# Layer one's second product in groups of 384 tokens over four rooms, with a new order of work

## The chip, the cores and the metric

The kernel runs on one core of a Trainium2 chip. The metric is the device time of one execution in microseconds (us), taken over three runs.

## The reference

Attention of 4 batches, 8 heads, 576 tokens, head size 64; half the heads see a window of 32 tokens, half every fourth token of 128. Its output, 2,304 tokens of 512, goes through two layers of products:

```python
def _moe_ref(x, w_in, w_out, g_ln):
    h = x @ w_in                                   # 2304x512 @ 512x1024
    h_max = np.max(h, axis=-1, keepdims=True)
    e = np.exp(h - h_max)
    sm = e / (np.sum(e, axis=-1, keepdims=True) + 1e-09)
    solu = h * sm
    mu = np.mean(solu, axis=-1, keepdims=True)
    var = np.mean((solu - mu) ** 2, axis=-1, keepdims=True)
    ln = (solu - mu) / np.sqrt(var + 1e-06) * g_ln
    return (ln @ w_out).astype(np.float32)         # 1024x512: the second product of layer one

def _moe2_ref(x, w_in, w_out):
    h = x @ w_in                                   # 512x2048
    g = h * (1.0 / (1.0 + np.exp(-1.702 * h)))
    return (g @ w_out).astype(np.float32)          # 2048x512
```

## The kernel before

Three parts overlap on one core. **Attention** goes by batch, five units of heads and tokens each: scores `s` (L268, with filler matmuls on `ident_b`, L250), softmax `t` on DVE, ACT and POOL, transposes `ptp` (L351), the product with v, `xt` (L381, L384), and copies `xr`. Loads of qk and v (L225, L231) are issued by SP. For two of a batch's units q, k and v lie, until attention ends, in room lent by the tiles `y1`, where layer one's results come later.

**Layer one** goes by tiles of 128 tokens, 18 of them. A tile's x is split into a high and a low fp32r half (`xh`, `xl`); `h` is 2 x 12 matmuls of 512 columns (L522); exp, the sums and the norm run on ACT, DVE and POOL in a tile `e`, of which there are three. Then `moe_lt` (L577) transposes e into PSUM, 2 x 4 matmuls, `moe_lnh` (L585, ACT or DVE) copies the high half out and `moe_lnl` (L588, DVE) subtracts the low one. The weights of layer one come in eight chunks (0 to 3 w_in, 4 to 7 w_out), as 64-bit numbers loaded by `fetch_w1` (L422) into rooms `w1r`, converted on ACT and DVE (L429, L437, L441), and split into `wi_h`, `wi_l` (L478, L491) and `wo_h`, `wo_l` (L485, L495). The rooms `w1r` and the transposed halves `lnh`, `lnl` share four slots "ln".

The second product, `moe_y` (L599), takes groups of YG = 256 tokens, two tiles. For each of 9 groups and 4 blocks `dm` of 128 outputs it makes 24 matmuls into one of four PSUM banks "B":

```python
for f in range(NF1):
    for j, (w, x) in enumerate(((wo_h, lnh), (wo_h, lnl), (wo_l, lnh))):
        nc.tensor.matmul(yps[g, dm][:, 0:n], w[:, f, ds_], x[:, f, 0:n],
                         start=(f == 0 and j == 0), stop=(f == NF1 - 1 and j == 2))
```

`moe_yc` (L604, ACT or DVE) copies the 256 columns into `y1`, tiles of TG = 512 tokens.

**Layer two** takes three passes of 768 tokens, each by seven products of half blocks (`hx`, `hz`, L721; `ox`, `oz`, L799; 384 columns a matmul). Its operands `yc` are sums and splits of pieces of y1 (L697, L704, L708), cut where a piece crosses two y1 tiles. Its weights are fetched while layer one runs, as 64-bit numbers (L629), converted, summed in fours (L638), split (L655, L659), stored to DRAM as `wdq`, `wdo` (L663) and loaded again later as `ws`, `wo`, `w`. A unit of this is listed in PARK: lists 1 and 2 use rooms in y1, list 3 rooms that open when attention has ended (`closed`). Kept units stay in `hl` tiles.

The order is written out. Every step is a work `add(rank, engine, cost, function, after, take, give)`; `in_order` walks the table ORDER, PICKS says which of a step's engines does it, and `emit` ties each engine's instructions to that order. So an engine, and SP's queue of loads, goes by the table, and semaphores between engines decide when each step starts. `plan_sequence` sets which steps follow which at first (`push_lt`, `push_y`), the wait lists `after` and the slots (SLOTS) which must.

Of the kernel before, what the change touches and what calls it, by code (L numbers as in the profile page):

```python
# [8 lines left out]
F32 = mybir.dt.float32  # L9
# [21 lines left out]
TG = 512  # L31
GROUPS = [(g * TG, min(TG, NT - g * TG)) for g in range((NT + TG - 1) // TG)]
NTILE = NT // P
YG = 256
NYG = NT // YG
# [131 lines left out]
def attention_moe_kernel(ctx, tc, qk, qk_last, v, v_last, masks, w_in, w_out, g_ln, w2_in, w2_out, out):  # L167
# [30 lines left out]
    lnp = m1_ctx.enter_context(tc.tile_pool(name="lnp", bufs=4))  # L198
# [393 lines left out]
    def moe_y(g, dm):  # L592
        n = YG
        yps[g, dm] = psB.tile([P, 512], F32, tag="B", name=f"y{g}_{dm}")
        lnh, lnl = lns[g]
        ds_ = slice(dm * P, dm * P + P)
        for f in range(NF1):
            for j, (w, x) in enumerate(((wo_h, lnh), (wo_h, lnl), (wo_l, lnh))):
                nc.tensor.matmul(yps[g, dm][:, 0:n], w[:, f, ds_], x[:, f, 0:n],  # L599
                                 start=(f == 0 and j == 0), stop=(f == NF1 - 1 and j == 2))  # L600

    def moe_yc(g, dm, copy):
        gg, c0 = g * YG // TG, g * YG % TG
        copy(y1[gg][:, dm, c0:c0 + YG], yps.pop((g, dm))[:, 0:YG])  # L604
# [273 lines left out]
    for what, i in LOADS:  # L878
# [12 lines left out]
        else:  # L891
            done["w", i] = add(r, "SP", 2 * W_T * f, lambda i=i: (fetch_w1(i, 0), fetch_w1(i, 1)), lag=2.2, take=("ln",))
# [39 lines left out]
    for c in range(8):  # L932
# [659 lines left out]
```

## Time and profile before

| | |
|---|---|
| median of three runs | 652.5 us (652.29 to 653.0) |
| the profiled execution | 652.41 us |
| its span in the profile | 650.6 us |
| granted clock of TensorE, mean | 0.994 |
| PE busy | 632.1 us, 97% |
| DVE, ACT, POOL busy | 69%, 54%, 45% |
| DMA moved | 163.56 MB, 251 GB/s in the mean |

The page shows one execution. "Busy" adds up an engine's instructions; the slices cut the span into 40 equal parts; the chain goes back from the last instruction, at each step to what released it. PE lines are matmuls, PEld lines loads of weights beside them, SPq lines the issue of transfers by SP. A matmul's record is longer than its distance to the next, since they are pipelined; what a matmul costs PE in a row is read from a run's length by its count.

### The profile page before, as it was taken

The page shows a single profiled execution, that of the slowest core. Times are in us where ns is not written, and L with a number is a line of the kernel's source. Part 1 is how long each engine was busy: PE and PEld are TensorE (multiplying, and loading weights), DVE is VectorE, ACT ScalarE, POOL GpSimd, SP SyncE. Part 2 cuts the span into 40 slices and gives each one's busy share as a digit, 9 for nine tenths or more (in the row PEclk, how much of TensorE's full clock was granted, in tenths as well). Part 3 has the DMA queues.
Part 4 walks back from the last instruction along what each step waited for, and adds up shares of the span by engine and source line. Part 5 has one row for each costly group of instructions (what it writes and reads, how often), then busy time and mean ns, then how long its engine had stood idle before and what let it go on. Part 6 is the DMA issues. An engine that isn't in the chain of part 4 may idle for free.

```text
span 650.6 us, 14875 instructions
## 1 busy us (share of the span) xinstructions
PE 632.1 (97%) x5878; PEld 594.6 (91%) x5878; DVE 448.1 (69%) x778; ACT 351.8 (54%) x766; POOL 292.9 (45%) x338
## 2 busy tenths in 40 slices
PE   6699999999999999999999999999999999999997
PEld 3478788889998989999999999999999999999997
DVE  4978789786846857796878879635477943447573
ACT  4677877755726565445656665333455531435552
POOL 3536563656557365555554215210535550224373
PEclk9989999999999999999999999999999999999999
DMA  8987428654537357877799999757899866779783
GB/s 337 394 287 303 172 85 282 225 168 174 162 128 255 146 174 247 320 230 228 283 346 379 358 329 314 227 198 265 264 295 286 301 221 226 244 245 341 251 255 111
DMA packets 65013, 163.56 MB, mean 251 GB/s; under 512 B 6960, under 2 KB 28592, under 8 KB 64944
## 3 DMA queue, kind: packets, MB, share of 16 engines
q1 hardware_dynamic: 64944, 162.62, 72.7%
q8 instruction: 46, 0.75, 0.5%
q14 instruction: 23, 0.19, 0.1%
HBM read 126.42 MB, written 36.18 MB: 250 GB/s over the span
## 4 chain that ended last, share of the span: by engine, by line
PE 89%; DMA 3%; DVE 3%; ACT 1%; issue 1%; POOL 0%; SPq 0%; POOLq 0%; ACTq 0%
PE y L599 16%; PE h L522 16%; PE hz L721 15%; PE oz L799 14%; PE hx L721 11%; PE ox L799 9%; PE lt L577 3%; PE xt L381 2%; PE ptp L351 1%; PE xt L384 1%; PE s L268 1%; DMA wo<-wdo 1%; DMA ws<-wdq 1%; DVE gs L767 1%; DMA wdo<-hl_('o', 3, 1)_1_5307 1%
## 5 line engine op out<-in xcount | busy, mean ns | idle before, releaser
L764 ACT CAST gs<-g 128x384 fp32r<-128x384 f32 x168 | 85.2, 514 | 70.6 <-PE oz L799 27.3
L767 POOL TENSOR_TENSOR gs<-g,gs 128x384 fp32r<-128x384 f32 x51 | 56.5, 1114 | 112.3 <-ACT gs L764 104.7
L721 PE MATMUL hz<-yc,ws 128*128 128x384 f32 x492 | 97.7, 334 | 0.0
L767 DVE TENSOR_TENSOR gs<-g,gs 128x384 fp32r<-128x384 f32 x117 | 75.3, 663 | 28.9 <-ACT gs L764 28.2
L721 PEld LDWEIGHTS hz<-yc,ws 128*128 128x128 f32 x492 | 86.5, 188 | 0.0
L599 PE MATMUL y<-lnh,wo_h 128*128 128x256 f32 x288 | 82.8, 288 | 0.0
L599 PE MATMUL y<-lnl,wo_h 128*128 128x256 f32 x288 | 81.4, 283 | 0.0
L599 PE MATMUL y<-lnh,wo_l 128*128 128x256 f32 x288 | 81.4, 283 | 0.0
L721 PE MATMUL hx<-yc,ws 128*128 128x384 f32 x369 | 74.9, 335 | 0.3 <-DMA ws<-wdq 0.3
L750 ACT ACTIVATE g<-g 128x384 f32<-128x384 f32 x72 | 36.6, 522 | 58.6 <-DVE g L740 40.6
L760 POOL TENSOR_TENSOR g<-g,g 128x384 f32<-128x384 f32 x34 | 38.5, 1136 | 65.3 <-ACT g L750 41.2
L721 PEld LDWEIGHTS hx<-yc,ws 128*128 128x128 f32 x369 | 64.8, 188 | 0.7 <-ACT hl_('q', 7, 1)_0_4958 L655 0.5
L522 PE MATMUL h<-wi_h,xh 128*128 128x512 f32 x144 | 59.3, 412 | 0.0
L799 PE MATMUL ox<-gs,wo 128*128 128x384 f32 x288 | 55.4, 337 | 1.1 <-DMA wo<-wdo 1.1
L522 PE MATMUL h<-wi_h,xl 128*128 128x512 f32 x144 | 56.4, 391 | 0.0
L522 PE MATMUL h<-wi_l,xh 128*128 128x512 f32 x144 | 56.3, 391 | 0.0
L599 PEld LDWEIGHTS y<-lnh,wo_h 128*128 128x128 f32 x288 | 55.0, 191 | 0.4
L599 PEld LDWEIGHTS y<-lnl,wo_h 128*128 128x128 f32 x288 | 55.1, 191 | 0.3
L799 PE MATMUL oz<-gs,wo 128*128 128x384 f32 x288 | 55.3, 336 | 0.0
L599 PEld LDWEIGHTS y<-lnh,wo_l 128*128 128x128 f32 x288 | 55.1, 191 | 0.0
L799 PE MATMUL oz<-gs,w 128*128 128x384 f32 x288 | 53.6, 337 | 0.5 <-DVE ou L811 0.5
L799 PEld LDWEIGHTS ox<-gs,wo 128*128 128x128 f32 x288 | 50.3, 188 | 1.5 <-DMA wo<-wdo 1.4
(397 smaller groups left out, 1315.8 us busy)
## 6 DMA issues: line engine op xcount, KB each, us to landing
wo<-wdo SPq DMA_DIRECT2D x48, 512.0 KB, 6.4
ws<-wdq SPq DMA_DIRECT2D x41, 512.0 KB, 6.0
w<-wdo SPq DMA_DIRECT2D x72, 256.0 KB, 5.6
ws<-wdq SPq DMA_DIRECT2D x41, 384.0 KB, 5.4
qk<-in_qk_dram SPq DMA_DIRECT2D x14, 528.0 KB, 6.4
v<-in_v_dram SPq DMA_DIRECT2D x14, 512.0 KB, 7.1
y<-in_w_in_dram SPq DMA_DIRECT2D x9, 512.0 KB, 5.1
wdq<-y SPq DMA_DIRECT2D x9, 512.0 KB, 3.9
```

What stands on the lines that cost most here:

```text
L268: nc.tensor.matmul(ps[QB * j:QB * j + QB, h, m * KW:m * KW + KW], q_[rows, c:c + QB], k_[rows, c:c + KW], start=not masked, stop=not maske ...
L351: nc.tensor.transpose(ps[:, j * P:j * P + P], t[:, 2 * j:2 * j + 2, :].rearrange("p m k -> p (m k)"), ident)
L381: nc.tensor.matmul(o, w, pt[rows, x:x + QB].rearrange("p (r t) -> p r t", r=4), start=True, stop=True, tile_position=(64 * par, 64 * h))
L522: nc.tensor.matmul(hps[i][:, half, :], x[:, kt, :], w[:, kt, fs], start=(kt == 0 and j == 0), stop=(kt == KT - 1 and j == 2))
L577: nc.tensor.transpose(ps[:, j, :], es[i][:, f * P:f * P + P], ident)
L599: nc.tensor.matmul(yps[g, dm][:, 0:n], w[:, f, ds_], x[:, f, 0:n], start=(f == 0 and j == 0), stop=(f == NF1 - 1 and j == 2))
L721: nc.tensor.matmul(ps[:, 0:TB2], quad_weights(p, q, m, kk, a), yc2[m][:, x, kk, :], start=(m < 4 and kk == 0 and i == 0), stop=(kk == 1 an ...
L750: nc.scalar.activation(g_tile(q, 0, 0) if (half, b) == (0, 0) else src, src, AF.Gelu_apprx_sigmoid)
L760: eng.tensor_tensor(o_block(jj, *o), o_block(jj, *x), o_block(jj, *y_), op)
L764: nc.scalar.copy(gsp[jj, m][:, 0], o_block(jj, half, b))
L767: eng.tensor_tensor(gsp[jj, m][:, 1], o_block(jj, half, b), f32(gsp[jj, m][:, 0]), ALU.subtract)
L799: nc.tensor.matmul(ps, w, gsp[jj, m][:, x], start=m < 4 and first and i == 0, stop=last and i == 2, skip_group_check=True)
```

## The change

`moe_y` takes groups of TG = 384 tokens, three tiles, so that there are 6 groups and 24 products of 24 matmuls. The transposed halves have one tile `ln_t` of four rooms, each for one tile of 128 tokens, high and low. An even group uses rooms 0, 1, 2, an odd one 3, 2, 1 (`ln_slot`): the first tile of a group goes to the room that the group before leaves out and waits for the group before that; the other two wait for the last product of the group before. The odd groups' tokens so lie in reverse order of tiles; the host turns them round in the output. The matmul's moving operand has 384 columns in three rooms, 128 in each. `ln_t` has the place of `w1_t`, four load slots for the eight chunks of w_in and w_out (`W_ORDER`, `W_SLOT`); the transposes of the first four tiles wait for all eight low halves.

The results lie in six tiles of 384 tokens, four of them in one tile `y1_early`. The lent room and the parked rooms lie in it at other places, list 2 splits into a room `park_hl` of attention's own, and one unit moves from list 2 to list 3. The wait for the units that borrow room goes from the y products to their copies. Layer two's pieces, 384 tokens wide, fall on whole y1 tiles. The tables ORDER and PICKS are new.

```diff
-TG = 512
-YG = 256
-NYG = NT // YG
+TG = 384
+NG = NT // TG
+GT = TG // P
...
-    y1 = {}
-    for g in range(3):
-        y1[g] = cpool.tile([P, KT, TG], F32, name=f"y1_{g}")
+    y1_early = cpool.tile([P, 4, KT, TG], F32, name="y1_early")
+    y1 = {g: y1_early[:, g] for g in range(4)}
...
-    lnp = m1_ctx.enter_context(tc.tile_pool(name="lnp", bufs=4))
+    lnp = m1_ctx.enter_context(tc.tile_pool(name="lnp", bufs=1))
+    w1_t = lnp.tile([P, 4, 2, 512, 2], U32, tag="ln", name="w1_t")
...
+    park_hl = ac.tile([P, 1024], F32R, name="park_hl")
+    parked = {1: (flat[:, 4096:5120], flat[:, 3072:4096].bitcast(F32R)), 2: (flat[:, 5120:6144], park_hl)}
...
-            lns[g] = (lnp.tile([P, NF1, YG], F32R, tag="ln", name=f"lnh{g}"),
-                      lnp.tile([P, NF1, YG], F32R, tag="ln", name=f"lnl{g}"))
+            ln_t = lnp.tile([P, 4, 2, NF1, P], F32R, tag="ln", name="ln_t")
...
-        lnh, lnl = lns[g]
+        lnh, lnl = (ln_t[:, g % 2:g % 2 + GT, which] for which in range(2))
...
-                nc.tensor.matmul(yps[g, dm][:, 0:n], w[:, f, ds_], x[:, f, 0:n],
+                nc.tensor.matmul(yps[g, dm][:, 0:TG].rearrange("p (t n) -> p t n", t=GT), w[:, f, ds_], x[:, :, f, :],
...
-            t = add(r, "PE", 0.37, lambda i=i, h=h2: moe_lt(i, h), [w, lt_of.get(i * P // YG), before_],
-                    take=("B", "ln", "ln") if i % 2 == 0 and h2 == 0 else ("B",), give=("e",) if h2 else ())
+            t = add(r, "PE", 0.37, lambda i=i, h=h2: moe_lt(i, h), [w, before_] + (list(lo.values()) if i <= GT else []), take=("B",),
+                    give=("e",) if h2 else ())
...
-                    + [end[n] for n in range(UB)] + ([closed] if g >= 6 else []) + (ys_ if dm == KT - 1 else []), take=("B",),
-                    give=("ln", "ln") if dm == KT - 1 else ())
+                    + (ys_ if dm == KT - 1 else []), take=("B",))
...
+                            [y] + [end[n] for n in range(UB)] + ([closed] if g == 4 else []), give=("B",), pick=0,
...
+    for i in range(GT, NTILE):
+        g = i // GT
+        free = y_done.get(g - 2 if i % GT == 0 else g - 1)
+        for h2 in range(2 if free else 0):
+            lt_of2[i, h2].after.append(free)
...
-                if k < 3:
+                for g in ((), (2, 3), (3,), ())[k]:
                     for dm in range(KT):
-                        yc[2 * k, dm].after.append(x)
-                        yc[2 * k + 1, dm].after.append(x)
+                        yc[g, dm].after.append(x)
+                if k == 2:
+                    closed.after.append(x)
...
+def ln_slot(i):
+
+    g, k = divmod(i, GT)
+    return 3 - k if g % 2 else k
...
+W_ORDER = (1, 3, 0, 2, 5, 7, 4, 6)
+W_SLOT = {1: 0, 3: 3, 0: 1, 2: 2, 5: 0, 7: 3, 4: 1, 6: 2}
...
-ORDER = [8, 1, 56, 57, 10, 58, 59, 60, 61, 5, 97, 98, 99, 9, 266, 267, 67, 268, 269, 270, 68, 62, 0, 46, 63, 100, 101,
...
-    got = _np.asarray(r.results[0]["out_0_dram"]).reshape(DM, B, 4, S // 4)
-    return _np.ascontiguousarray(got.transpose(1, 3, 2, 0)).reshape(NT, DM)
+    got = _np.array(r.results[0]["out_0_dram"]).reshape(DM, NG, GT, P)
+    got[:, 1::2] = got[:, 1::2, ::-1].copy()
+    return _np.ascontiguousarray(got.reshape(DM, B, 4, S // 4).transpose(1, 3, 2, 0)).reshape(NT, DM)
```

How the order moves, at three places. In these rows a line number is that of the kernel in question; behind it stand the operation, out<-in and the tile.

SP's queue at the start, before (`y_0` to `y_2` are lent rooms in y1, `w1r` the chunks of layer one's weights, `in_v` the v of batch 0):

```order
L222 DMA y_1_78<-in_qk_dram 128x544
L422 DMA w1r_275<-in_w_in_dram 128x1024 x2
L237 DMA qkl_336<-in_qk_last_dram 128x640
L239 DMA vl_338<-in_v_last_dram 128x512
L422 DMA w1r_392<-in_w_in_dram 128x1024 x2
L231 DMA v_420<-in_v_dram 128x1024
L231 DMA v_428<-in_v_dram 128x1024
L422 DMA w1r_446<-in_w_in_dram 128x1024 x2
L225 DMA qk_549<-in_qk_dram 128x1056
L231 DMA y_1_78<-in_v_dram 128x1024
L231 DMA y_2_79<-in_v_dram 128x1024
```

and with the change, where `y_early` are the lent rooms and `w_t` the chunks:

```order
L425 DMA w_t<-in_w_in_dram 128x1024 x2
L228 DMA qk_316<-in_qk_dram 128x1056
L234 DMA y_early<-in_v_dram 128x1024
L425 DMA w_t<-in_w_in_dram 128x1024 x4
L240 DMA qkl_442<-in_qk_last_dram 128x640
L242 DMA vl_444<-in_v_last_dram 128x512
L234 DMA v_450<-in_v_dram 128x1024
L234 DMA v_456<-in_v_dram 128x1024
L234 DMA y_early<-in_v_dram 128x1024
L425 DMA w_t<-in_w_in_dram 128x1024 x2
```

Before, two v loads of batch 0 stood ahead of the fourth w_in chunk (`w1r_446`) and two behind it. Now one stands ahead of the second and third chunk, and all of them ahead of the fourth.

DVE around the first transposes' low halves, before (`wo_l` are the low halves of w_out, `lnl` those of the transposed tiles, `y_1`, `y_2`, parked units under conversion):

```order
L337 TENSOR_SCALAR sx_1318<-sx_1318 128x8
L338 RECIPROCAL sx_1318<-sx_1318 128x8
L588 TENSOR_TENSOR lnl_1215<-lt_0_1216,lnh_1214 128x4x128
L588 TENSOR_TENSOR lnl_1215<-lt_1_1274,lnh_1214 128x4x128
...
L588 TENSOR_TENSOR lnl_1215<-lt_1_1464,lnh_1214 128x4x128
...
L585 CAST lnh_1214<-lt_0_1437 128x4x128
L588 TENSOR_TENSOR lnl_1215<-lt_0_1437,lnh_1214 128x4x128
L441 SCALAR_TENSOR_TENSOR w1r_911<-w1r_911 128x1024
L483 TENSOR_SCALAR wo_h<-w1r_911,g_sb 128x512 x2
L495 SCALAR_TENSOR_TENSOR wo_l<-w1r_827,g_sb,wo_h 128x512 x2
...
L495 SCALAR_TENSOR_TENSOR wo_l<-w1r_911,g_sb,wo_h 128x512 x2
```

and with the change:

```order
L360 COPY pt_1263<-ptp_1241 128x512
L498 SCALAR_TENSOR_TENSOR wo_l<-w_t,g_sb,wo_h 128x512 x4
L444 SCALAR_TENSOR_TENSOR y_early<-y_early 128x512
L498 SCALAR_TENSOR_TENSOR wo_l<-w_t,g_sb,wo_h 128x512 x2
...
L545 SCALAR_TENSOR_TENSOR e_1311,mu_1368<-h_1091,e_1311 128x1024
...
L533 TENSOR_REDUCE nm_1391<-h_1246 128x1
...
L589 TENSOR_TENSOR ln_t<-lt_0_1380,ln_t 128x512
L589 TENSOR_TENSOR ln_t<-lt_1_1429,ln_t 128x512
...
L589 TENSOR_TENSOR ln_t<-lt_1_1386,ln_t 128x512
```

The last four low halves of w_out stood behind the first tiles' low halves; now all of them stand ahead of the first.

PE at the end of layer one, before (of each y product the first matmul is shown; `lt` are the transposes, `hx`, `hz` the first products of layer two):

```order
L577 MATMUL lt_1_4251<-ident,e_3882 128x128 x4
L577 MATMUL lt_1_4259<-ident,e_4069 128x128 x4
L599 MATMUL y_3_4266<-lnh_3978,wo_h 128x256
...
L599 MATMUL y_1_4302<-lnh_4164,wo_h 128x256
...
L599 MATMUL y_0_4340<-lnh_4164,wo_h 128x256
...
L599 MATMUL y_2_4373<-lnh_4164,wo_h 128x256
...
L721 MATMUL hx_0_0_4403<-yc_0_4023,ws_0_0_0_4025 128x384 x3
L721 MATMUL hx_0_0_4403<-yc_0_4023,ws_0_1_0_4074 128x384 x3
L599 MATMUL y_3_4416<-lnh_4164,wo_h 128x256
...
L721 MATMUL hx_0_1_4455<-yc_1_4333,ws_0_0_1_4161 128x384 x3
```

and with the change:

```order
L599 MATMUL y_3_3866<-ln_t,wo_h 128x384 x2
...
L579 MATMUL lt_0_3905<-ident,e_3694 128x128 x4
L579 MATMUL lt_0_3912<-ident,e_3784 128x128 x4
L579 MATMUL lt_1_3918<-ident,e_3784 128x128 x4
L579 MATMUL lt_1_3926<-ident,e_3694 128x128 x4
L720 MATMUL hx_0_0_3931<-yc_0_3810,ws_0_0_0_3864 128x384 x3
L720 MATMUL hx_0_0_3931<-yc_0_3810,ws_0_1_0_3847 128x384 x3
L720 MATMUL hz_0_2_3943<-yc_2_3748,ws_0_0_1_3714 128x384 x3
L720 MATMUL hz_0_2_3943<-yc_2_3748,ws_0_1_1_3854 128x384 x3
L599 MATMUL y_0_3955<-ln_t,wo_h 128x384 x2
...
L599 MATMUL y_1_3992<-ln_t,wo_h 128x384 x2
...
L720 MATMUL hx_0_1_4114<-yc_1_4020,ws_0_0_1_3714 128x384 x3
```

Before, the last product of the group ahead stood behind the last transposes, and layer two's first product between the last two y products. Now the last 16 transposes stand together, 12 matmuls of layer two behind them, and then the last group's four products in a row.

## Rows read from the trace of the kernel before

**Rows 1.** The page: busy time by engine, and what DMA moved in 40 slices of 16.3 us.

```profile
PE 632.1 (97%) x5878; PEld 594.6 (91%) x5878; DVE 448.1 (69%) x778; ACT 351.8 (54%) x766; POOL 292.9 (45%) x338
...
GB/s 337 394 287 303 172 85 282 225 168 174 162 128 255 146 174 247 320 230 228 283 346 379 358 329 314 227 198 265 264 295 286 301 221 226 244 245 341 251 255 111
```

**Rows 2.** The page: the chain that ended last, by engine and by line.

```profile
PE 89%; DMA 3%; DVE 3%; ACT 1%; issue 1%; POOL 0%; SPq 0%; POOLq 0%; ACTq 0%
PE y L599 16%; PE h L522 16%; PE hz L721 15%; PE oz L799 14%; PE hx L721 11%; PE ox L799 9%; PE lt L577 3%; PE xt L381 2%; PE ptp L351 1%; PE xt L384 1%; PE s L268 1%; DMA wo<-wdo 1%; DMA ws<-wdq 1%; DVE gs L767 1%; DMA wdo<-hl_('o', 3, 1)_1_5307 1%
```

**Rows 3.** Stretches: length, busy us (instructions) by engine, granted clock, DMA share, GB/s.

```profile
0.00:50.00 50.00, 37.57 (x964) 25.92 (x965) 35.86 (x58) 31.43 (x78) 20.29 (x21) 0.93 0.93 340
50.00:100.00 50.00, 49.41 (x856) 41.66 (x854) 40.49 (x72) 37.66 (x88) 28.41 (x40) 1.00 0.47 175
150.00:200.00 50.00, 50.00 (x393) 45.94 (x392) 31.65 (x61) 26.35 (x52) 29.18 (x42) 1.00 0.52 180
300.00:350.00 50.00, 49.75 (x287) 49.46 (x286) 37.52 (x73) 26.98 (x55) 27.66 (x31) 1.00 0.89 317
350.00:400.00 50.00, 48.94 (x281) 48.30 (x280) 42.87 (x76) 31.35 (x64) 14.97 (x13) 1.00 1.00 340
```

**Rows 4.** The chain in order of time: start us, us, what, matmuls.

```profile
87.23 1.06 PE xt L384 x64
88.29 2.95 PE h L522 x12
...
258.25 0.44 PE lt L577 x4
...
278.97 11.51 PE y L599 x96
...
330.84 6.33 DMA ws<-wdq
...
372.81 7.65 DMA wo<-wdo
...
387.02 8.32 PE ox L799 x48
```

**Rows 5.** Groups on PE: line, operation, names, shapes, count, busy us, mean ns, idle.

```profile
L599 PE MATMUL y<-lnh,wo_h 128*128 128x256 f32 x288 | 82.8, 288 | 0.0
...
L522 PE MATMUL h<-wi_h,xl 128*128 128x512 f32 x144 | 56.4, 391 | 0.0
```

**Rows 6.** Timeline of PE: the filler matmuls before a masked score.

```profile
26.74 1.04 PE L250 MATMUL s<-ident_b 128*128 128x512 bf16 x4
```

**Rows 7.** Timeline at the start: start us, us, engine, line, operation, [idle, releaser].

```profile
27.64 1.22 ACT L437 ACTIVATE w1r<-w1r 128x1024 uint32<-128x1024 uint8 x1
...
28.69 1.22 ACT L429 ACTIVATE w1r<-w1r 128x1024 f32<-128x1024 f32 x1
...
31.42 1.49 DVE L441 SCALAR_TENSOR_TENSOR w1r<-w1r 128x1024 uint32<-128x1024 uint32 x1
...
32.94 0.69 DVE L478 CAST wi_h<-w1r 128x1024 fp32r<-128x1024 f32 x1
...
33.71 2.41 POOL L491 TENSOR_TENSOR wi_l<-w1r,wi_h 128x1024 fp32r<-128x1024 f32 x1 [1.89 <-DVE wi_h L478]
...
38.16 0.94 PE L522 MATMUL h<-wi_h,xh 128*128 128x512 f32 x1
```

**Rows 8.** One line's instructions: ns min/median/max, first and last start us.

```profile
L495 DVE SCALAR_TENSOR_TENSOR wo_l<-w1r,g_sb,wo_h x8: 721/743/750, 45.0 to 87.1; 128x512 fp32r<-128x512 f32 x8
...
L577 PE MATMUL lt<-ident,e x144: 270/272/329, 65.8 to 278.7; 128*128 128x128 f32 x144
...
L585 ACT CAST lnh<-lt x22: 558/587/592, 69.7 to 279.0; 128x512 fp32r<-128x512 f32 x22
L585 DVE CAST lnh<-lt x14: 676/691/692, 81.0 to 278.6; 128x512 fp32r<-128x512 f32 x14
...
L588 DVE TENSOR_TENSOR lnl<-lt,lnh x36: 640/686/693, 70.9 to 279.9; 128x512 fp32r<-128x512 f32 x36
```

More of the change, by code (lines that the diff above doesn't have):

```diff
@@ L580, in ln_part @@
     def ln_part(i, h2, which):
-        t0 = (i * P) % YG
-        return lns[i * P // YG][which][:, 4 * h2:4 * h2 + 4, t0:t0 + P]
+        return ln_t[:, ln_slot(i), which, 4 * h2:4 * h2 + 4, :]
     def moe_lnh(i, h2, copy):
@@ L891, in attention_moe_kernel @@
         else:
-            done["w", i] = add(r, "SP", 2 * W_T * f, lambda i=i: (fetch_w1(i, 0), fetch_w1(i, 1)), lag=2.2, take=("ln",))
+            done["w", i] = add(r, "SP", 2 * W_T * f, lambda i=i: (fetch_w1(i, 0), fetch_w1(i, 1)), lag=2.2)
     end = {}
@@ L938, in attention_moe_kernel @@
                           ("POOL", 2.0 if c < 4 else 2.2, lambda c=c: split_hi(c, nc.gpsimd))])
-        lo[c] = add(r, "DVE", 1.22 if c < 4 else 1.42, lambda c=c: split_lo(c), [hi[c]], give=("ln",), port=True,
+        lo[c] = add(r, "DVE", 1.22 if c < 4 else 1.42, lambda c=c: split_lo(c), [hi[c]], port=True,
                     also=[("POOL", 2.45, lambda c=c: split_lo(c, nc.gpsimd))][:c < 4], pick=int(c in LO_POOL))
+    slot_lo = {}
+    for c in W_ORDER:
+        if W_SLOT[c] in slot_lo:
+            done["w", c].after.append(slot_lo[W_SLOT[c]])
+        slot_lo[W_SLOT[c]] = lo[c]
+    lt_of2 = {}
     yc, lnl, h_of, xh_of, lt_of, solu = {}, {}, {}, {}, {}, []
@@ L976, in attention_moe_kernel @@
             lnl[i, h2] = add(r, "DVE", 0.68, lambda i=i, h=h2: moe_lnl(i, h), [t], give=("B",))
-    for g in range(NYG):
+    y_done = {}
+    for g in range(NG):
         ys_ = []
@@ L1016, in split @@
                 def split(copy, k=k, u=u, part=part):
-                    t = flat[k][:, 1024:2048].bitcast(F32R) if k < 3 else hl_tile(
+                    t = parked[k][1] if k < 3 else hl_tile(
                         f"hl_{u}_{part}", hi_now[u, part], hl_end[u, part])
@@ L1040, in add_y @@
     def add_y(r, p, steps):
-        src = [yc[g, dm] for g in range(3 * p, 3 * p + 3) for dm in range(KT)]
+        src = [yc[g, dm] for g in range(2 * p, 2 * p + 2) for dm in range(KT)]
         free = list(y_free)
@@ L1077, in attention_moe_kernel @@
     y_free, last_g = [], {}
-    add_y(at["y", 8, 0] - 0.5, 0, 0.01)
+    add_y(at["y", NG - 1, 0] - 0.5, 0, 0.01)
     for m in range(7):
@@ L1275, in push_lt @@
             to.append(("lt", k))
-            if k % 2:
-                owed.extend((k // 2, dm) for dm in range(KT))
+            if k % GT == GT - 1:
+                owed.extend((k // GT, dm) for dm in range(KT))
         def push_y(k):
```

48 lines of the change are left out of this document (24 added, 24 removed), and 293 rows, old and new, of tables (ORDER, PICKS).

## The prediction

> **What bounds the kernel now.** I read the page first, then the chain in order of time, then stretches of 50 us, then single instructions. The page says that TensorE is busy for 632.1 of 650.6 us [rows 1], and the chain that ended last runs over PE for 89%, with the y matmuls as its largest line, 16% [rows 2]. So a microsecond of PE work taken away is worth a microsecond, wherever no other wait takes its place. The stretches show where that could fail. In the first 50 us PE is busy for 37.57 us at a granted clock of 0.93, and the DMA engines are taken for 0.93 of the time: loads and softmax set the pace there, not matmuls. From 50 us on PE is full, at clock 1.00. Between 300 and 400 us it is still nearly full (49.75 and 48.94 of 50), but the DMA share is 0.89 and 1.00 [rows 3]. There the chain does leave PE for the reload of parked weights, 6.33 and 7.65 us [rows 4], so that this is the second place where a gain can be lost.
>
> The sum is made against the profiled execution: 652.41 us, of which 650.6 are the span and 1.8 lie around it; the median of the three runs shown is 652.5, 0.1 above.
>
> **Part 1, larger groups.** A y product of 96 matmuls of 256 columns takes 11.51 us, 119.9 ns each [rows 4]. At 2.4 GHz, which the clock of 1.00 is, 256 columns are 106.7 ns; 13.2 ns are paid per matmul. 48 matmuls of 384 columns in layer two take 8.32 us, 173.3 ns each [rows 4]; 384 columns are 160, so again 13.3 ns are paid. The same weights, products and columns go through either way, in 864 matmuls now (three groups of 288, [rows 5]) and 576 then: 864 x 119.9 = 103.6 us, 576 x 173.3 = 99.8 us. **The change saves 3.8 us** here if the new operand streams as the old one does; 288 x 13.25 is the same figure. The weight loads lie beside the matmuls, and there are 288 fewer.
>
> The skill differs. The Trainium skill, "TensorE: Matmul & The Clock Gate", section "Back-to-back issue gap", gives a warm gap of N/2.4 + 2.5 ns for a matmul taken alone. By it 288 matmuls would be worth 0.7 us; the two rows above, at both sizes, disagree with it (13.2 and 13.3 ns), and the sum goes by the rows.
>
> The operand is new in one way: its 384 columns lie in three rooms, three runs of 128. The trace of before has no such fp32 matmul. The nearest row is the filler on ident_b, whose 512 columns are four runs over the same 128: four take 1.04 us [rows 6]. With a last record of 0.39 us, as the 512-column h matmuls have [rows 5], the three before it are 0.217 us apart, and 512 columns at 2.4 GHz are 0.213. I take nothing for the runs; the other end is a rival.
>
> **Part 2, copies and fewer pieces.** 36 copies of y into y1 become 24 larger ones, and layer two's y pieces aren't cut any more: less on ACT and DVE, which are 54% and 69% busy and off the chain. Zero, hidden behind PE. The copies, not the matmuls, now wait for the parked rooms that lie in y1; the closest is the third group's copy, which stands one to two y products (24 x 173.3 ns = 4.2 us each) behind the last store of room 1 in the order, and that store takes some us to land. It holds one of four B banks meanwhile: zero, with 2 us as the bad end.
>
> **Part 3, start.** SP now issues batch 0's v loads ahead of the last w_in chunk. Adding up the transfers' sizes in the order of issue, the last of these v's ends at 8,528 KB (before: 10,080), the last w_in chunk at 9,552 KB (8,528). With 337 and 394 GB/s in the first two slices of 16.3 us [rows 1], these v's landed at about 28.5 us and now would at 24.5, while the last w_in chunk goes from 24.5 to 27.2. What stands between a w_in chunk and its use: 1.22 + 1.22 us on ACT, 1.49 and 0.69 on DVE, then a low part of 1.2 on DVE or 2.41 on POOL [rows 7], 5.8 us at best; as queued in the trace, from 27.64 to 36.1, 8.5. So the first h, at 38.16 now [rows 7], could start between 33.0 and 35.7: 2.5 to 5 us earlier. But batch 1's v loads then end 1,024 to 1,552 KB later than before (15,236 and 17,876 KB against 14,212 and 16,324), at 287 to 303 GB/s [rows 1] 3.5 to 5.4 us later, and the transfers are what is short up to 60 us. Most of the lead is waited away again; I take a third of 4 us, **-1.3**, with ends -4 (all kept) and +2 (the later loads cost more than was gained).
>
> **Part 4, first transposes.** The four rooms share their place with the load slots of w_in and w_out. Before, first transposes needed two of four slots free; now the first copy out of them, on ACT, has to wait until all eight splits are done. In the trace the low halves of w_out on DVE run from 45.0 to 87.1 us, the first transpose is at 65.8 [rows 8]. The last two chunks must move ahead. Between the last of them and the first transposes the order leaves PE two sets of 64 xt matmuls and 12 of h, 2 x 1.06 + 2.95 = 5.1 us [rows 4], while the copies need it done only behind the transposes: zero, and the price of a miss is a rival.
>
> **Part 5, end of layer one.** The last tiles' 16 transposes now stand together, with 12 matmuls of layer two (12 x 173.3 ns = 2.1 us) between them and the last group, where before 24 to 72 y matmuls stood behind each pair. Four copies of 0.59 or 0.69 us and four DVE subtractions of 0.69 [rows 8] must come out of that: 4 x 0.69 + 0.59 = 3.3 us from the first transposes' end, and the last three sets of transposes take 3 x 0.44 [rows 4] themselves: 1.3 + 2.1 = 3.4. About even; **+0.3**, ends 0 and 0.8.
>
> **Part 6, layer two's weights.** PARK 2 gives one unit to PARK 3, and ahead of the last xt, which opens PARK 3's rooms, stand two more h halves (2 x 2.95), 6 y products of 4.16 us for 8 of 2.88, and two more lt (2 x 0.44): about 8.7 us more PE work. From there to the end of layer one the fetches catch up: by their sizes in the order of issue, both programs have asked for the same 64,708 KB when the last y ends. Zero, ends -1.3 (PE's idle time in 300 to 400 us, [rows 3], going away) and +4.8 (rival 1).
>
> Sum: 652.4 - 3.8 - 1.3 + 0.3 = **647.6 us**.
>
> **Rivals.**
> 1. *The transfers take it back.* Between 320 and 400 us the weights' reloads run at a share of 1.0; if bytes alone set when hx and ox can start, PE arrives 4.8 us early and waits. For it: the chain's DMA pieces [rows 4]. Against: at 150 to 200 us the share is 0.52 [rows 3], so there is room to park earlier. Gain back in full: about 652.4; in half: 650. Chance 0.14.
> 2. *Short runs stream slower* (slower than before). Each y matmul crosses two borders between rooms; if a border cost what a new matmul does, 13 ns, 576 x 2 x 13 = 15 us come back on PE, in y alone: 662.6. From 4.2 ns a border (4.8 / 1,152) nothing is gained, from 5.3 it is slower. Against: the filler's 0.217 us over four runs [rows 6]. Chance 0.06.
> 3. *The first transposes' copies wait for w_out.* The two chunks carried forward are 2 x (1.49 + 2 x 0.74) = 5.9 us of DVE [rows 7, 8] into 45 to 65 us, where DVE, busy for 40.49 of 50 us [rows 3], has some 4 us free. If they end 5.9 us late, three tiles hold their rooms, exp and h stand behind them, PE waits as long, and then for the first copy and three subtractions in a row, 0.59 + 3 x 0.69 = 2.7 us: 656.2. It passes the old time from 4.8 us of waiting in all. Chance 0.06.
> 4. *Cost goes by columns.* If the 13 ns grew with the columns, 576 x 179.9 ns would be 103.6 us again and nothing were saved in y: 651.4. The rows at 256 and 384 columns speak against it. Chance 0.02. The Trainium skill's gap (page and section above) leaves nearly as little, 0.7 us: 650.7 by that estimate.
>
> **How the numbers follow.** My forecast has 0.72, from 643.8 (start's lead kept, -2.7, and PE's waits gone, -1.3, less a little) to 650. This kernel's runs can tell about 0.2%, 1.3 us, from no change. Rival 1 gives 0.03 to faster, 0.10 to same and 0.01 to slower; rivals 2 and 3 are slower; rival 4 is same. Faster 0.75, same 0.12, slower 0.13. The range, 643.8 to 653.5, leaves out most of rivals 2 and 3, and a little below.
>
> **What would show it.** Right: y matmuls of 384 columns, 173 to 174 ns apart in the chain; first h at 33 to 36 us; no wait of PE between 45 and 75 us on a copy out of lt; layer one's end some 5 us sooner, and hx, ox waiting for ws, wo as little as before. Wrong: y at over 178 ns apart (rival 2, 4); PE idle on an lnh or on DVE's w_out split (rival 3); more than 2 us more of PE idle time between 300 and 400 us on ws or wo (rival 1).

## The result, and the profile after

The change is slower: **658.33 us** (median of 7 runs, 656.88 to 661.63) against 652.45 us (7 runs, 652.29 to 655.52) of the kernel before on the same chip, ratio 1.0091, 95% interval 1.0064 to 1.0119. The forecast was 647.6 us with a range up to 653.5; the result lies above it. The profiled execution took 656.88 us, of which 655.1 are the span: 4.5 us more than the span of before, which was 650.6. It is the quickest of the seven, so the traces explain 4.5 us of the 5.9 between the medians.

The page after: busy time by engine, and the chain that ended last.

```profile
PE 632.4 (97%) x5587; PEld 590.4 (90%) x5587; DVE 448.4 (68%) x736; ACT 353.8 (54%) x757; POOL 307.1 (47%) x348
...
PE 81%; DVE 6%; DMA 5%; issue 3%; POOL 2%; ACT 1%; SPq 1%; ACTq 0%; DVEq 0%; POOLq 0%
PE y L599 15%; PE h L525 15%; PE hz L720 14%; PE oz L798 10%; PE hx L720 10%; PE ox L798 8%; PE lt L579 3%; DMA wo<-wdo 2%; DVE gs L766 2%; PE s L271 2%; PE xt L384 1%; PE xt L387 1%; DMA v<-in_v_dram 1%; PE ptp L354 1%; DMA wdo<-hl_('o', 3, 1)_1_4964 1%
```

PE's busy time hides the story: it is 0.3 us more than before [rows 1], although PE executes 291 matmuls fewer. (The ends of matmuls are modelled, so their busy time is rough.) The chain tells it better. PE has 81% of it, 89% before [rows 2]; DVE has 6% for 3%, and gs, line L766, 2% for 1%. POOL, with no share before, has 2%, and 307.1 us of work for 292.9.

Before's operands `lnh` and `lnl` are called `ln_t` here, and the tiles of y that lend their room to attention `y_early`. The larger groups, in the chain in order of time (start us, us, what, matmuls) and in the groups on PE:

```profile
255.71 12.51 PE y L599 x72
...
272.83 1.75 PE lt L579 x16
...
276.69 16.67 PE y L599 x96
```

```profile
L599 PE MATMUL y<-ln_t,wo_h 128*128 128x384 f32 x384 | 98.6, 337 | 0.0
...
L599 PE MATMUL y<-ln_t,wo_l 128*128 128x384 f32 x192 | 64.3, 335 | 0.0
```

16.67 / 96 and 12.51 / 72 are 173.7 ns for a matmul of 384 columns, what layer two's matmuls of that size take [rows 4]. 576 x 173.7 = 100.1 us, against 864 x 119.9 = 103.6 before: the 3.5 us are really saved.

The stretches (length, busy us and instructions by engine, granted clock, DMA share, GB/s), of after:

```profile
0.00:50.00 50.00, 37.47 (x988) 25.97 (x988) 37.21 (x55) 31.72 (x76) 17.71 (x24) 0.90 0.90 338
50.00:100.00 50.00, 49.26 (x817) 39.61 (x812) 44.05 (x73) 40.18 (x100) 32.57 (x42) 1.00 0.66 238
300.00:350.00 50.00, 49.39 (x283) 48.75 (x282) 37.18 (x67) 27.60 (x58) 28.19 (x34) 1.00 0.90 312
350.00:400.00 50.00, 48.33 (x274) 47.02 (x273) 41.51 (x73) 30.00 (x60) 11.89 (x11) 1.00 0.99 338
...
500.00:600.00 100.00, 97.11 (x557) 96.47 (x557) 57.43 (x92) 38.92 (x84) 34.31 (x27) 1.00 0.79 257
```

and the last one, of before:

```profile
500.00:600.00 100.00, 100.00 (x577) 100.00 (x577) 56.00 (x95) 39.74 (x86) 34.55 (x31) 1.00 0.77 261
```

Up to 100 us PE is as busy as before, between 300 and 400 PE is idle for 2.28 us where it was 1.31 [rows 3], and between 500 and 600, where before had no idle time at all, 2.89 us are missing, at full clock and with the DMA engines no busier. What PE waited for from 300 us to the end (us in total, times, longest), after and then before:

```profile
PE oz L798 <- DVE gs L766: 3.0, 2, 2.6
PE oz L798 <- DMA wo<-wdo: 0.9, 2, 0.5
PE ox L798 <- DMA wo<-wdo: 0.7, 1, 0.7
PE hx L720 <- DMA ws<-wdq: 0.5, 1, 0.5
```

```profile
PE ox L799 <- DMA wo<-wdo: 1.1, 1, 1.1
PE oz L799 <- DVE ou L811: 0.5, 1, 0.5
PE hx L721 <- DMA ws<-wdq: 0.3, 1, 0.3
```

A wait for `gs` on DVE, 2.6 us of it in one piece, is new; `gs` is layer two's activated operand, which DVE and GpSimd finish in turn. The three engines there (start us, us, engine, line, operation, [idle, releaser]), DVE, GpSimd and PE:

```profile
517.73 0.56 DVE L766 TENSOR_TENSOR gs<-g,gs 128x384 fp32r<-128x384 f32 x1 [1.84 <-ACT gs L763]
518.82 1.60 DVE L766 TENSOR_TENSOR gs<-g,gs 128x384 fp32r<-128x384 f32 x1 [0.53 <-ACT gs L763]
520.34 2.60 DVE L696 TENSOR_TENSOR y<-y,y 128x768 f32<-128x768 f32 x1
522.87 2.16 DVE L766 TENSOR_TENSOR gs<-g,gs 128x384 fp32r<-128x384 f32 x1
```

```profile
517.77 4.35 POOL L707 TENSOR_TENSOR yc<-y,yc 128x768 fp32r<-128x768 f32 x2
522.21 2.41 POOL L696 TENSOR_TENSOR y<-y 128x768 f32<-128x768 f32 x1
```

```profile
525.09 1.15 PE L798 MATMUL oz<-gs,w 128*128 128x384 f32 x5 [2.56 <-DVE gs L766]
```

The same operation of DVE takes 0.56, 1.60 and 2.16 us. The long ones end shortly after a GpSimd instruction ends: the two `yc` (768 elements per lane, taken as equally long) are over at about 519.9 and at 522.12, the sum of y at 524.62; DVE's ends are 520.42, 522.94 and 525.03. So each of the three ends 0.41 to 0.82 us behind GpSimd's instruction, a little less than its usual time, as if it had stood until that one was through. PE runs out of `gs` at 522.53 and waits 2.56 us. The Trainium skill, "SBUF — State Buffer", section "Who interferes with whom", says that a VectorE instruction with two SBUF inputs contends with a GpSimd instruction that reads SBUF, for ports that they share and only one of them can hold. The trace agrees: 1.60 and 2.16 us for the `gs` that come behind a GpSimd instruction, 0.56 for the one that began just ahead of it (517.73 and 517.77 us).

A stretched `gs` is not new. All of DVE's `gs` (ns min/median/max, first and last start us), after and then before:

```profile
L766 DVE TENSOR_TENSOR gs<-g,gs x109: 542/557/2161, 320.6 to 646.7; 128x384 fp32r<-128x384 f32 x109
```

```profile
L767 DVE TENSOR_TENSOR gs<-g,gs x117: 542/558/1647, 312.8 to 642.2; 128x384 fp32r<-128x384 f32 x117
```

Over 0.8 us take 22 of the 109, and 20 of the 117 before, where the list above has no wait of PE for `gs`. What is new is three stretched instructions in a row on DVE, at a place where PE needs what they make.

**Where the 4.5 us came from.** To place the loss I took each matmul of both traces at its usual distance (119.8, 173.5 and 229.2 ns for 256, 384 and 512 columns, 110 for a transpose, 14.9 and 16.6 for one of the small ones in s and xt, fillers at zero) and compared the work not yet started at the same times. A positive number is the change's lead in us; the kernels of the experiments are there too, each from its one profiled execution.

| us | 90 | 150 | 290 | 340 | 400 | 500 | 540 | 640 |
|---|---|---|---|---|---|---|---|---|
| change | 2.9 | 2.8 | 2.1 | 1.6 | 0.2 | -1.0 | -3.6 | -4.7 |
| change again (e4) | 2.7 | 2.4 | 1.6 | 1.7 | 1.9 | 0.7 | -3.5 | -4.3 |
| three y pieces to DVE (e3) | 1.8 | 1.7 | 0.9 | 1.0 | 0.0 | -1.2 | -1.0 | -1.7 |
| before's late order (e1) | 2.9 | 2.7 | 1.9 | 2.3 | 0.7 | 0.5 | 0.7 | 0.2 |
| before's order after y (e2) | -0.7 | -1.0 | -1.6 | -2.6 | -1.7 | -1.9 | -1.9 | -2.3 |

The change has 3.5 us less to do from the first moment, so a lead of 2.9 at 90 us says that the start gave nothing and cost about 0.7. 0.8 us go between 90 and 290, in small pieces where PE passes from one kind of matmul to another: 1.5 us in 85 such passages, 0.7 in 92 before. From 290 us on, that is in layer two, 6.8 us are lost, 2.6 of them between 500 and 540 us (4.2 in the second execution).

### The profile page after: what moved, and what is told of

It is laid out like the page before. It is cut to its first block, busy times and chain, and to the rows that moved or that the text cites. A ratio compares the mean times of both kernels' runs of the same rounds, so it can differ in the third digit from the quotient of the medians.

```text
span 655.1 us, 14276 instructions
## 1 busy us (share of the span) xinstructions
PE 632.4 (97%) x5587; PEld 590.4 (90%) x5587; DVE 448.4 (68%) x736; ACT 353.8 (54%) x757; POOL 307.1 (47%) x348
## 4 chain that ended last, share of the span: by engine, by line
PE 81%; DVE 6%; DMA 5%; issue 3%; POOL 2%; ACT 1%; SPq 1%; ACTq 0%; DVEq 0%; POOLq 0%
PE y L599 15%; PE h L525 15%; PE hz L720 14%; PE oz L798 10%; PE hx L720 10%; PE ox L798 8%; PE lt L579 3%; DMA wo<-wdo 2%; DVE gs L766 2%; PE s L271 2%; PE xt L384 1%; PE xt L387 1%; DMA v<-in_v_dram 1%; PE ptp L354 1%; DMA wdo<-hl_('o', 3, 1)_1_4964 1%
## 5 line engine op out<-in xcount | busy, mean ns | idle before, releaser
L763 ACT CAST gs<-g 128x384 fp32r<-128x384 f32 x168 | 84.9, 513 | 73.9 <-PE oz L798 33.9
L766 POOL TENSOR_TENSOR gs<-g,gs 128x384 fp32r<-128x384 f32 x59 | 67.2, 1143 | 98.2 <-ACT gs L763 87.3
L599 PE MATMUL y<-ln_t,wo_h 128*128 128x384 f32 x384 | 98.6, 337 | 0.0
L766 DVE TENSOR_TENSOR gs<-g,gs 128x384 fp32r<-128x384 f32 x109 | 74.4, 699 | 33.5 <-ACT gs L763 33.0
L759 POOL TENSOR_TENSOR g<-g,g 128x384 f32<-128x384 f32 x38 | 42.2, 1117 | 80.2 <-ACT g L749 51.8
L599 PEld LDWEIGHTS y<-ln_t,wo_h 128*128 128x128 f32 x384 | 68.9, 188 | 0.5
L599 PE MATMUL y<-ln_t,wo_l 128*128 128x384 f32 x192 | 64.3, 335 | 0.0
L798 PEld LDWEIGHTS oz<-gs,w 128*128 128x128 f32 x288 | 50.0, 188 | 4.1 <-DVE gs L766 3.6
L798 PEld LDWEIGHTS oz<-gs,wo 128*128 128x128 f32 x288 | 50.2, 188 | 2.2 <-ACT hl_('o', 3, 0)_0_4868 L654 0.7
L759 DVE TENSOR_TENSOR g<-g,g 128x384 f32<-128x384 f32 x58 | 40.4, 701 | 14.0 <-POOL gs L766 8.2
```

The source lines that it names most:

```text
L599: nc.tensor.matmul(yps[g, dm][:, 0:TG].rearrange("p (t n) -> p t n", t=GT), w[:, f, ds_], x[:, :, f, :], start=(f == 0 and j == 0), stop=( ...
L759: eng.tensor_tensor(o_block(jj, *o), o_block(jj, *x), o_block(jj, *y_), op)
L763: nc.scalar.copy(gsp[jj, m][:, 0], o_block(jj, half, b))
L766: eng.tensor_tensor(gsp[jj, m][:, 1], o_block(jj, half, b), f32(gsp[jj, m][:, 0]), ALU.subtract)
L798: nc.tensor.matmul(ps, w, gsp[jj, m][:, x], start=m < 4 and first and i == 0, stop=last and i == 2, skip_group_check=True)
```

## The experiments

The rival causes were these. *Layer two's order*: the new search puts y's low halves and sums (L707, L696) on GpSimd beside DVE's `gs`. *The weights*: their reloads between 300 and 400 us. *The start*: four rooms force loads and conversions into a worse order, or the granted clock, which lies below 1.00 for part of the first 40 us, holds it back. Ratios below are to the kernel before on the same chip, with 95% intervals; its medians were 653.70 us beside e1 to e4, 653.70 beside e5 to e7, 652.77 beside e8 to e10 and 653.50 beside e11.

**e4_change_again.** No edit: the change a second time, on the chip of e1 to e3.

> The changed kernel as it is, beside the others on one chip: 657.5 to 659 us. The same lags of PE show again at about 300, 380 and 522 us if they belong to the order, and stand elsewhere if they are chance.

Measured: 659.67 us (6 runs, 656.45 to 660.63), ratio 1.0076 (1.0053 to 1.0100). PE's waits from 300 us on:

```profile
PE oz L798 <- DVE gs L766: 3.0, 2, 2.6
PE oz L798 <- DMA wo<-wdo: 1.0, 1, 1.0
```

The same wait with the same lengths: it belongs to the order, not to one execution. The waits on reloads differ (1.0 against 2.1 us), and the lag between 300 and 400 us does not come again: the lead is 1.6 at 290 and 1.9 at 400. The wait's price differs too. In the first trace the granted clock stayed at 1.00 behind it; here, after PE had stood for 2.56 us, it is near its lower level of 1.2 GHz for most of 4 us (stretches as above):

```profile
524.00:526.00 2.00, 2.00 (x8) 2.00 (x7) 1.78 (x3) 0.00 (x0) 2.00 (x3) 0.52 0.24 26
526.00:528.00 2.00, 2.00 (x10) 2.00 (x9) 0.78 (x1) 0.48 (x1) 1.65 (x1) 0.63 0.90 287
```

4 us at 0.58 are 1.7 us of the full clock lost, and the lead falls by 4.2 us between 500 and 540, where it fell by 2.6 in the first trace.

**e1_order2_late.** The change, with before's order and choice of engine from the last parked unit on. On GpSimd, for example, the two low halves that ran together at 517.77 us are gone, and another comes alone later:

```diff
-L707 TENSOR_TENSOR yc_6_6090<-y_5_3713,yc_6_6090 128x768
-L707 TENSOR_TENSOR yc_4_6181<-y_4_2798,yc_4_6181 128x768
...
+L707 TENSOR_TENSOR yc_2_6412<-y_5_3713,yc_2_6412 128x768
```

> The changed kernel, but from the last parked weight on (about 370 us) every step of layer two stands in the order, and on the engines, of the kernel before; the larger groups, the rooms and all before that stay. Theory A (the new order of layer two's steps loses time: DVE and GpSimd pieces of y stand beside the gs operands that oz waits for): of the 5.4 us that PE falls behind after 380 us, 4 to 5 come back; 653 to 654.5 us where the change has 658.3, PE's wait for DVE gs at 522 us gone. Theory B (the earlier end of layer one only brings PE sooner to late weights): the order is not at fault, the time stays at 657 to 659.

Measured: 653.71 us (12 runs), ratio 1.0008 (0.9986 to 1.0030). The stretch from 500 to 600 us:

```profile
500.00:600.00 100.00, 100.00 (x578) 100.00 (x577) 56.42 (x95) 39.47 (x82) 33.96 (x29) 1.00 0.78 262
```

PE is full again, as before, and the loss against before is gone. By the medians all of the 6.0 us to e4 lie in the order of layer two, by the traces 4.7 (span 650.4 for 655.1). Two waits of 1.1 us for reloads of wo stay.

**e2_order2_all.** The change, with before's order and engines for everything behind the last copy of y; only layer one and attention keep the new order.

```diff
-ORDER, PICKS: as in the change
+ORDER, PICKS: as in the change up to the last copy of y, then as before
```

> As the run before, but from the last y copy on (about 295 us), with the remaining parked units too, everything in the order and on the engines of the kernel before. Theory A: the 1.4 us that PE loses between 300 and 360 us come back as well, 651 to 653 us. Theory B: PE waits more for ws and wo between 300 and 400 us than before, and the time is within 1 us of the changed kernel's.

Measured: 652.38 us (12 runs), ratio 0.9982 (0.9963 to 1.0001). It is the best version with groups of 384, and not shown to be faster than before. In its trace the waits on reloads come to 0.9 us, but the lead is -0.7 at 90 us already, 3.6 below the change's, with the same steps up to there: the start differs that much between executions. The granted clock of the first 60 us is 0.86 in this one, 0.91 in the change's; whether the clock or what lowers it takes the time is not shown.

**e3_y_on_dve.** The change, with two low halves of y and one sum moved from GpSimd to DVE; nothing else.

```diff
 PICKS = {
-1979: 1,
-1984: 1,
-1985: 1,
```

> The changed kernel with three y pieces of the last pass (two low halves, one sum of 768 numbers a lane) on DVE where they ran on GpSimd at 517 to 525 us; nothing else moves. Theory A1 (DVE and GpSimd hold each other up: DVE's gs took 1.60 and 2.16 us there, its y sum 2.60, where 0.56 and 0.95 are usual): although DVE gets more work, its pieces return to 0.56 and 0.95 us, and PE's wait of 2.6 us for gs falls below 0.5: 655.5 to 656.5 us where the change has 658.3. Theory A2 (DVE simply has too much in its queue there): DVE is later still, by 3 x 0.95 us, and the time goes to 660 to 661.

Measured: 654.17 us (12 runs), ratio 1.0011 (0.9992 to 1.0031), 5.5 us below e4. DVE in that place, and PE's wait for `gs`:

```profile
518.39 0.95 DVE L707 TENSOR_TENSOR yc<-y,yc 128x768 fp32r<-128x768 f32 x1
519.26 0.55 DVE L766 TENSOR_TENSOR gs<-g,gs 128x384 fp32r<-128x384 f32 x1
519.73 0.95 DVE L696 TENSOR_TENSOR y<-y,y 128x768 f32<-128x768 f32 x1
520.60 0.55 DVE L766 TENSOR_TENSOR gs<-g,gs 128x384 fp32r<-128x384 f32 x1
521.07 0.95 DVE L707 TENSOR_TENSOR yc<-y,yc 128x768 fp32r<-128x768 f32 x1
```

```profile
PE oz L798 <- DVE gs L766: 0.4, 1, 0.4
```

Giving DVE more to do makes the kernel faster: with the two `yc` of 0.95 us on DVE itself, `gs` is back at 0.55 and the y sum falls from 2.60 to 0.95. Three instructions out of some 14,000 are thus the largest single cause. The traces show 2.7 us of it (the span fell from 654.9 or 655.1 to 652.2); the medians show 5.5, about twice the 2 to 3 that the trace had led me to expect. The profiled executions of the change are at the low end of its runs. The longer executions are mostly those with the lower granted clock: the five of the change and of e4 over 660 us have 0.984 to 0.987 in the mean, and e3's five from 655.5 us on have 0.981 to 0.987, its other seven 0.989 to 0.995. Taken apart there, the medians of e4 and e3 are 4.5 us (below 0.989) and 4.9 us (from 0.989 on) apart, so the three pieces cost that much at like clocks too. What makes it more than the 2.7 of the traces is not shown: the other executions have no trace.

**e6_before_y_on_pool.** The counter-test: the kernel before, with one low half of y and the two parts of one sum moved to GpSimd.

```diff
 PICKS = {
+2007: 1, 2012: 1, 2013: 1,
```

> The kernel before with three y pieces of the last pass (a low half of 768 numbers a lane, the two parts of one sum) moved from DVE to GpSimd at about 515 us; nothing else differs. Theory A1 (the two engines hold each other up): the DVE gs beside them go from 0.56 to over 1.2 us, and PE waits for gs at about 515 to 522 us, 1 to 3 us: 653.7 becomes 655 to 657. If GpSimd's pieces only cost GpSimd, DVE gets lighter and the time stays within 0.5 us.

Measured: 654.39 us (12 runs), ratio 1.0008 (0.9988 to 1.0028): +0.7 us, below the forecast and no proof by time. The stretching is there, DVE first and GpSimd beside it:

```profile
508.90 3.88 DVE L767 TENSOR_TENSOR gs<-g,gs 128x384 fp32r<-128x384 f32 x3
```

```profile
509.74 2.16 POOL L708 TENSOR_TENSOR yc<-y,yc 128x768 fp32r<-128x768 f32 x1
```

The same three `gs` take 2.23 us in the kernel before, so one is stretched there already, beside another GpSimd instruction:

```profile
508.26 2.23 DVE L767 TENSOR_TENSOR gs<-g,gs 128x384 fp32r<-128x384 f32 x3
```

PE waited only 0.5 us for them: here one low half stood alone, with enough `gs` ready. So the counter-test shows the stretching, and not its price: a collision costs what PE has to wait for by it, 0.5 us here and 2.6 in the change.

**e5_both_ends_before.** e2, with before's order also for the steps ahead of the first y; the conversions of the last two w_out chunks had to be pulled ahead of the first transposes. On SP, for example:

```diff
-L228 DMA qk_316<-in_qk_dram 128x1056
-L234 DMA y_early<-in_v_dram 128x1024
-L425 DMA w_t<-in_w_in_dram 128x1024 x4
+L228 DMA qk_252<-in_qk_dram 128x1056
+L224 DMA y_early<-in_qk_dram 128x512
+L225 DMA y_early<-in_qk_dram 128x544
```

> As e2 (everything from the last y copy on in the order of the kernel before), and the steps ahead of the first y product, too, in the order and on the engines of the kernel before: loads, attention, tiles. Only the conversions of the last two w_out chunks stand earlier than there, as the rooms demand. Theory C (the start's new order loses PE time, because batch 1's v loads land later): PE is at 60 to 100 us no further behind the kernel before than 0.5 us in work, where e2 was behind by 3 to 4; 649 to 651 us, 1.5 to 3 below e2's 652.4. Theory D (the start is set by the transfers in either order, or the transposes' wait for all of w_out takes the place): no gain over e2, 652 to 654; if the wait for w_out bites, PE idles at 60 to 75 us and it is 654 to 656.

Measured: 671.17 us (6 runs), ratio 1.0261 (1.0228 to 1.0294). PE from 90 to 120 us, and its longest wait on layer one's transposes:

```profile
90.00:120.00 30.00, 22.22 (x207) 17.16 (x206) 20.39 (x35) 16.48 (x46) 13.25 (x20) 0.83 0.42 151
```

```profile
PE lt L579 <- POOL e L568: 4.6, 1, 4.6
```

By the count of the table PE is 3.3 us behind before at 90 us and 15 at 120. Neither theory's time came true. The run shows that before's sequence, with the conversions moved by hand, does not suit the four rooms; it does not show that the new start is the best one or what the larger groups cost there. `e` was late because GpSimd waited 5.25 us for `sq` on ACT, and in this order `sq` stands on ACT behind an `xh` that waited 2.80 us for PE's h.

**e7_start_before_y_dve.** e5's start, with everything from the first y on as in e3:

```diff
-ORDER, PICKS up to the first y: as in e3
+ORDER, PICKS up to the first y: as in e5
```

> The changed kernel with the start of the kernel before, as in e5, and three y pieces of the last pass on DVE, as in e3; from the first y product on its own order otherwise. Theory C: 1.5 to 3 us below e3's 654.2, 651 to 652.7. Theory D: 654 to 656.

Measured: 670.03 us (6 runs), ratio 1.0266 (1.0221 to 1.0311). The same loss, again outside both forecasts; it tells no more than e5.

**e8_e2_fillers, e9_e2_many_fillers, e10_before_fillers.** More filler matmuls on `ident_b`, to hold the granted clock at the start: e2 with 55 and with 105 instead of 25, and before with 63 instead of 28.

```diff
-        for _ in range(min(4, int(STIR * plan.gap / 4))):
+        for _ in range(min(8, int(STIR * plan.gap / 4))):
-STIR = 7
+STIR = 14
```

(e9 has 14 and 24 in these places.)

> e2 with more filler matmuls in the gaps of the start: 55 where e2 has 25, up to eight in a gap where it was four (512 columns each, 0.217 us at full clock, 0.43 at half). Theory E (the new start lets the granted clock fall earlier, to 0.67 between 15 and 25 us and again at 30 to 35, and PE pays for it): the clock between 15 and 40 us rises above 0.9, PE has done 1 to 2 us more work at 60 us than e2 and e4, 650.5 to 651.5 us against e2's 652.4. Theory C (loads and softmax set the start, the clock only shows it): clock up, time within 0.7 us of e2's.

> As e8 with 105 fillers, up to 14 in a gap. Theory E: no better than e8, since fillers that outlast a gap hold up the work behind them: 651 to 653 us. Theory C: they delay softmax's inputs and the time is 653 to 656.

> The control for e8: the kernel before with 63 fillers where it has 28, up to eight in a gap. Its clock falls only between 30 and 40 us (0.71 and 0.61). Theory E: a smaller gain, 0 to 1 us, 652.7 to 653.7. Theory C: no change beyond 0.7 us.

Measured: e8 658.85 us, ratio 1.0095 (1.0069 to 1.0121); e9 659.32, 1.0094 (1.0071 to 1.0118); e10 657.64, 1.0064 (1.0046 to 1.0081). The stretch from 25 to 40 us, in e8 and in e9:

```profile
25.00:40.00 15.00, 10.80 (x215) 7.41 (x216) 12.15 (x17) 7.34 (x16) 6.15 (x5) 0.66 0.68 245
```

```profile
25.00:40.00 15.00, 12.38 (x270) 7.93 (x269) 14.56 (x18) 9.94 (x19) 8.16 (x5) 1.00 0.67 238
```

All three are slower by 5 to 7 us, which neither theory had. In e8 the clock is held from 15 to 25 us (1.00, where e2 has 0.69) and not behind it; in e9 it is at 1.00 in both stretches, and the kernel is as slow as e8. So fillers that stand on PE ahead of scores and transposes cost more than the clock gives back. What the lower clock costs by itself these runs can't tell, since they change both.

**e11_e2_v_earlier.** e2, with one load of batch 1's v ahead of the first w_out chunk and one ahead of the other three, since the chain of e2 waits for v until 51.4 us. On SP:

```diff
+L234 DMA v_586<-in_v_dram 128x1024
 L425 DMA w_t<-in_w_out_dram 128x1024 x2
...
+L234 DMA v_734<-in_v_dram 128x1024
+L425 DMA w_t<-in_w_out_dram 128x1024 x6
```

> e2 with two of batch 1's v loads moved forward in SP's queue: one ahead of the first w_out chunk, which waits there for its room until 28.8 us while the DMA engines fall to half, one ahead of the chunks that follow. Theory C (the late v loads cost the start its lead): the xt product that waited until 48.8 us for its v starts 1 us or more earlier, PE has done 1 to 2 us more work at 60 us, 650.5 to 651.5 us against e2's 652.4. If the wait only moves to the next load or to w_out (rival 3), the time is 652 to 654.

Measured: 652.60 us (12 runs), ratio 0.9991 (0.9974 to 1.0008). The chain in order of time:

```profile
42.45 6.12 DMA w_t<-in_w_out_dram
...
49.65 1.11 ACT w_t L440
...
52.31 1.14 PE xt L384 x64
```

The first of the two v now lands at 30.58 us instead of 51.40. The wait moves to a w_out chunk, which lands at 48.57 us, and to its conversion on ACT, behind which stands what xt needs; xt begins at 52.31 us, no earlier than e2's 51.54. So the forecast's second case came. An ACT order with the conversion further back was not tried.

## Why the prediction was wrong

**Part 1 was right.** -3.5 us for -3.8, at 173.7 ns a matmul, and the operand's three runs of 128 columns cost nothing: rivals 2 and 4 are out. The gap of N/2.4 + 2.5 ns that the Trainium skill, "TensorE: Matmul & The Clock Gate", section "Back-to-back issue gap", gives for a matmul taken alone would have made it 0.7. This case differs from it: 119.9 and 173.7 ns in a row are 13.2 and 13.7 ns over N/2.4.

**Part 2 is the step that failed**: "layer two's y pieces aren't cut any more: less on ACT and DVE ... Zero, hidden behind PE." It looked at how much work there is and how busy DVE and ACT are, not at who does it and beside what. The diff's new table of picks put three of these pieces of the last pass on GpSimd. DVE's busy time hardly changed (448.4 us for 448.1); what changed is that three DVE instructions in a row were held up, by up to 1.65 us each, in a place where PE had no `gs` in reserve. Moving the three back (e3) gives 2.7 us by the traces and 5.5 by the medians. With the rest of layer two's order it is 4.7 us by the traces (e1: 650.4 for 655.1) and 6.0 by the medians; what in the rest of the order costs is not shown. No rival named it: all four looked at layer one or at transfers. With that term the sum would have lost its sign.

**Part 3 was wrong in size, and in what it let the first h wait for.** The first h came at 37.89 us, not at 33.0 to 35.7 (before 38.16, [rows 7]):

```profile
37.89 0.54 PE L525 MATMUL h<-wi_h,xh 128*128 128x512 f32 x1
```

The sum counted from the last w_in chunk, at 27.2 us; it lands at 28.90. But the first h needs only two of the four: three are split by 32.19 us, and the last one at 41.59, while h is running. What came last was x, split into its halves from 35.17 to 37.39 us. DVE was held up ahead of that, too: a `wi_l`, 1.23 us otherwise, took 3.31 beside one on GpSimd. Then SP stands from 20.3 to 28.8 us at a chunk that waits for its room, with later loads behind it, and the DMA share falls to 0.53 between 25 and 30 us, where the sum took the queue as always full. Batch 1's first two v land at 48.84 and 55.72 us, 3.7 and 4.5 later than before, as foreseen, and xt waits for the first:

```profile
41.00 7.84 DMA v<-in_v_dram
```

So the -1.3 was +0.7 in this execution, by the lead at 90 us, and +0.7 to +4.3 in the others with the same steps up to there (e1 to e4).

**Part 4 was right.** The low halves of w_out now run from 52.1 to 73.9 us, and the first copy out of the transposes follows at 80.6 (columns as in [rows 8]):

```profile
L498 DVE SCALAR_TENSOR_TENSOR wo_l<-w_t,g_sb,wo_h x8: 737/745/1334, 52.1 to 73.9; 128x512 fp32r<-128x512 f32 x8
```

```profile
L586 ACT CAST ln_t<-lt x23: 569/588/617, 80.6 to 274.7; 128x512 fp32r<-128x512 f32 x23
```

Rival 3 didn't happen in the change; in e5, with before's start, PE did stand for 4.6 us at a transpose whose `e` was late, of the rival's kind but not by the wait that it named.

**Part 5** was 0 for +0.3: the chain shows 16 transposes at 272.83 and the last y at 276.69, with no wait of PE between them.

**Part 6 and rival 1** were right in direction. PE waits 2.1 us for ws and wo where it waited 1.4, and is idle 1.0 us more between 300 and 400. That is well short of the 4.8 us of the rival.

Against the terms, then: -3.5 for y, 0.7 for the start, 0.8 lost in small pieces between 90 and 290 us (not tried), and 6.8 lost in layer two, which make 4.8; the spans differ by 4.5. Without the bad order (e1, e2, e3) the kernel ties with before. Where the 3.5 us of y went there is shown only in part: in e1 1.6 us are gone by 290, and most of the rest by 400, where the wo reloads are waited for; in e2 and e3 the start took more. The granted clock bears on it: it is 0.989 or more in all 29 runs of before beside them, and in 8, 8 and 7 of their 12. Those have medians of 652.8, 651.8 and 652.9 us, 0.8 to 1.9 below before's 653.7; the others 656.2, 654.9 and 655.9. So a part of the 3.5 is there when the clock holds, and whether the clock takes the rest, or what lowers it, stays open.

## What to carry to other kernels

A change that comes with a newly searched order is two changes: cost the order as well, above all which engine gets each vector instruction and what runs beside it on the other one. Busy shares don't show collisions between VectorE and GpSimd; compare the same operation's shortest and longest duration, and ask whether PE holds a reserve of what the stretched instruction makes: the kernel before has 20 stretched `gs`, and from 300 us on no wait of PE for one is listed. Where such a collision sits on the path, moving a few instructions back (here three, 5.5 us by the medians) is a cheaper test than a new search.

## What was not expected of the hardware

- A DVE instruction of 0.55 us can take 2.16 us, and one of 0.95 us 2.60, beside a GpSimd instruction of some 2.2 us on 768 elements per lane.
- Holding the granted clock at the start by fillers cost more than it gave: 80 more fillers brought it from 0.75 to 1.00 between 25 and 40 us, and the time rose by 6.9 us (e9 against e2).
- One wait of PE can have two prices: behind the same 2.56 us the granted clock stayed at 1.00 in one execution and was 0.52 and 0.63 for 4 us in the other (e4), 1.7 us more.
- Matmuls of 384 columns whose operand lies in three separate rooms of 128 are as fast, 173.7 ns, as those with one run of 384, 173.3 [rows 4].
- The same steps up to 90 us ended 3.6 us apart in two executions (the change's and e2's, with granted clocks of 0.94 and 0.91 up to there), more than what many experiments are meant to show.
